# The first loads and the first matmuls of a gated attention and token-mixing kernel: another order of the DMA queues, another order of the first projection

## The chip, the cores and the metric

The kernel runs on one core of one Trainium2 chip. The metric is the device time of one execution in microseconds (us). A core has five engines with instruction streams of their own: TensorE (PE) multiplies matrices into the eight banks of PSUM, VectorE (DVE) and ScalarE (ACT) compute on SBUF and PSUM, GpSimd (POOL) does little here, and SyncE (SP) issues most of the DMAs. ACT issues DMAs as well. The engines wait for one another, and for DMAs, through semaphores.

## The reference

One input x of 2048 rows and 512 columns goes two ways, and a gate mixes the results. Way A is an attention with 32 heads of 16 columns, in which a row sees itself and seven earlier rows, two apart; way B is a layer norm and a two-layer perceptron over the rows (tokens) instead of the columns.

```python
def reference(A_x, A_wqkv, A_wo, B_x, B_w1, B_b1, B_w2, B_b2, gate_w):
    x = A_x
    g = sigmoid((x * gate_w).sum(-1, keepdims=True))
    # A: q, k, v = x @ wqkv, split in 32 heads of 16
    #    row s sees the rows s, s-2, ..., s-14: softmax(q . k / 4), times v, then @ wo
    # B: h = layernorm(x)
    #    u = gelu(einsum("bsd,sf->bdf", h, w1) + b1)
    #    y = (einsum("bdf,fs->bds", u, w2) + b2) transposed to (b, s, d)
    return g * a + (1 - g) * b
```

All inputs are bfloat16; wqkv is 512 x 1536, wo 512 x 512, w1 2048 x 1792, w2 1792 x 2048.

## The kernel before

The kernel first computes q, k and v with x transposed (XT, four blocks of 512 rows: block 0 to block 3) as the moving operand and columns of wqkv as weights. Then DVE multiplies q and shifted k (L690), PE sums over a head's columns (L698), ACT and DVE do the softmax, PE does the first layer of the perceptron (L812) and the second (L862), and at last the output projection wo (L878), after which DVE mixes both ways (L899) and SP stores.

Nothing loops on the chip. A list of operations is written out in Python (`A(engine, function, duration, reads, writes, ...)`, `sch.dma(queue, ...)`), and a small planner in the same file (`_Sched`) puts them in an order for each engine. It goes by the durations given, by priorities (`prio`), by dependencies from `reads` and `writes`, by `order` edges that fix an order without a wait, and for some DMAs by a time of landing that is given by hand (`lands`). From the order it works out the waits. So a DMA's `lands` and an operation's duration decide nothing on the chip but the order.

The stage that matters here is the first 15 us.

- **Columns 0 to 127 of block 0.** SP loads them as they lie (XP, `d_xp`, L479: 512 pieces of 256 bytes). PE transposes them by matmuls against an identity (`f_tr`, L545, operations `tr0` and `tr1`), ACT evicts one half (`ev_tra`, L555) and DVE the other (`ev_trb`, L557).
- **Columns 128 to 511 of block 0** come by a transposing DMA (`ld_xt0`, L473). Blocks 1 to 3 come by transposing DMAs of all four column quarters (`ld_xt`, L460).
- **The weights.** `ld_w(tn, d0, n, q)` (L447) loads n quarters (of 128 rows) of Wq, Wk or Wv (tn 0, 1, 2), from quarter d0 on, by queue q. ACT's queue issues Wq's quarters 0 and 1 as its first work, SP's the rest: after `d_xp` and the transposing DMA come Wq's quarters 2 and 3, Wk's 0 and 1 together, Wk's 2 and 3 together, X's tiles 0 and 1 (`ld_x`, L439, for the layer norm), block 1, and X's tiles 2 and 3. The later ones wait for the landing of a DMA some places ahead (`throttle`).
- **Warm-up.** While nothing has landed, PE multiplies constants: six matmuls of 512 columns and one of 256 (`f_warm`, L537) ahead of the transposes, and one of 512 behind them.
- **The first projection.** q and k of block 0 are eight tiles (four column groups each), in eight PSUM banks, and each is the sum of four matmuls, over the quarters d = 0 to 3 (`f_proj`, L619). Before, PE goes over the quarters for q's four banks first (16 matmuls), then for k's four banks (16 matmuls), two quarters of one bank at a time.
- **Evictions.** ACT evicts a bank as soon as its four quarters are summed: L627 for q, L630 for k and v. After block 0 the projections of blocks 1 to 3 use banks 0 to 3 in turn, so each has to be evicted before it is used again.
- **ACT's table.** ACT loads a function table (1.28 us) ahead of its first activation; before, that is `ev_tra`, behind the two DMA issues.
- **DVE** takes the statistics of X's tiles 0 to 3 (L574) ahead of its first product of q and k (L690), which needs q and k of blocks 0 and 1 for one column group. That order is written out (`chain`, L959).

Of the kernel before, what the change touches and what calls it, by code (L numbers as in the profile page):

```python
# [6 lines left out]
FP32 = mybir.dt.float32  # L7
U8 = mybir.dt.uint8
ALU = mybir.AluOpType
AF = mybir.ActivationFunctionType  # L10
# [3 lines left out]
D = 512  # L14
# [319 lines left out]
def bass_gated_mix__sliding_local_dilated__mixer_token_mlp__prompt_kernel(nc, A_x, A_wqkv, A_wo, B_x, B_w1, B_b1, B_w2, B_b2, gate_w, out, dbg=None):  # L334
    with contextlib.ExitStack() as es:
# [3 lines left out]
        sch = _Sched()  # L339
# [3 lines left out]
        wqkv_v = A_wqkv.rearrange("(dt p) c -> p dt c", p=128)  # L343
# [7 lines left out]
        WQKV = view("WQKV", BF16, [(3 * D, 4), (1, 3 * D)])  # L351
# [26 lines left out]
        def small(n):  # L378
            v_ = view("SMALL", FP32, [(1, n)], extra=so[0])
            so[0] += n  # L380
            return v_
# [5 lines left out]
        SD = small(NST)  # L387
# [14 lines left out]
        def col(v_, i):  # L402
            return bass.AP(v_.tensor, v_.offset + i, [list(v_.ap[0]), [1, 1]])
# [11 lines left out]
        A = sch.add  # L415
# [12 lines left out]
        def mk_dma(dst, src):  # L428
            return lambda e: e.dma_start(dst, src)

        init_dmas = []

        def throttle():
            return [init_dmas[-5]] if len(init_dmas) >= 5 else []

        def prev_dma():
            return [init_dmas[-1]] if init_dmas else []

        def ld_x(t0, n, q="sp"):  # L439
            ds = sch.dsem("x%d" % t0)  # L440
            op = sch.dma(q, mk_dma(X[:, t0:t0 + n, :], xv[:, t0:t0 + n, :]), n * 128 * D * 2, ds,
                         writes=["x%d" % t for t in range(t0, t0 + n)], deps=throttle() if q == "sp" else [], after=prev_dma() if q == "sp" else [], name="d_x%d" % t0)
            if q == "sp":
                init_dmas.append(op)
            return op

        def ld_w(tn, d0, n, q="sp"):  # L447
            ds = sch.dsem("wqkv%d_%d" % (tn, d0))
            op = sch.dma(q, mk_dma(WQKV[:, d0:d0 + n, tn * D:(tn + 1) * D], wqkv_v[:, d0:d0 + n, tn * D:(tn + 1) * D]),
                         n * 128 * D * 2, ds, writes=["wqkv%d_%d" % (tn, dt) for dt in range(d0, d0 + n)],  # L450
                         deps=throttle() if q == "sp" and n == 4 else [], after=prev_dma() if q == "sp" else [],
                         issue=0.65 if n == 4 else 0.45, name="d_wp%d_%d" % (tn, d0))
            if q == "sp":
                init_dmas.append(op)
            return op

        def ld_xt(sb):
            ds = sch.dsem("xt%d" % sb)
            dst = XT[:, :, sb * 512:(sb + 1) * 512]
            op = sch.dma("sp", lambda e: e.dma_start_transpose(dst, x2d[sb * 512:(sb + 1) * 512, :]), 512 * D * 2, ds,  # L460
                         writes=["xt_%d" % t for t in range(4 * sb, 4 * sb + 4)], deps=throttle(), after=prev_dma(), name="d_xt%d" % sb)
            init_dmas.append(op)
# [4 lines left out]
        def xt_of(sb, d0=0, d1=4):  # L467
            return XT0[d0:d1] + (XT0[4:] if d0 == 0 else []) if sb == 0 else ["xt_%d" % t for t in range(4 * sb, 4 * sb + 4)]

        def ld_xt0():  # L470
            ds = sch.dsem("xt0")
            dst = XT[:, 1:4, 0:512]
            op = sch.dma("sp", lambda e: e.dma_start_transpose(dst, x2d[0:512, 128:512]), 512 * 384 * 2, ds, issue=1.25,  # L473
                         writes=XT0[1:4], after=prev_dma(), name="d_xt0")
            init_dmas.append(op)
            return op

        XP = view("OUTS", BF16, [(128, 4), (1, 128)])
        d_xp = sch.dma("sp", mk_dma(XP, xv[:, 0:4, 0:128]), 512 * 128 * 2, sch.dsem("xp"), writes=["outs0"], issue=0.4, name="d_xp")  # L479
        d_xp.lands = 3.9  # L480
        init_dmas.append(d_xp)

        first_loads = [ld_w(0, 0, 1, "act"), ld_xt0(), ld_w(0, 1, 1, "act"), ld_w(0, 2, 1), ld_w(0, 3, 1), ld_w(1, 0, 2), ld_w(1, 2, 2),
                       ld_x(0, 2)]
        ld_xt(1)
        first_loads.append(init_dmas[-1])
        for op_, t_ in zip(first_loads, (3.5, 5.7, 5.0, 6.3, 6.7, 7.6, 8.6, 9.4, 11.0)):
            op_.lands = t_
            op_.deps.clear()
        first_loads[2].order.add(first_loads[0])  # L490
        init_dmas[:] = [first_loads[1]] + first_loads[5:]
        ld_x(2, 2)
        ld_x(4, 4)
        ld_xt(2)
# [6 lines left out]
        def ld_w1(j):  # L501
# [4 lines left out]
            if j < 4:  # L506
# [8 lines left out]
                       writes=["wo"], deps=throttle(), after=prev_dma(), name="d_wo")  # L515
# [4 lines left out]
        for i_, (v_, n_) in enumerate(((B_b1, NFT), (B_b2, NST))):  # L520
            vr = v_.rearrange("(t q j) -> q t j", q=4, j=32)
            for q_ in range(4):
                sch.dma("sp", mk_dma(psub(BR, 32 * q_, n_, 32 * i_, [(1, 32)]), vr[q_]), n_ * 64, ds_b, reads=["br"],
                        writes=["br_%d_%d" % (i_, q_)], deps=throttle(), after=prev_dma(), name="d_b_%d_%d" % (i_, q_), issue=0.45)
        d_w1.append(ld_w1(3))
        A("dve", lambda e: e.transpose(out=BT, in_=BR), 0.2, reads=["br_%d_%d" % (i_, q_) for i_ in range(2) for q_ in range(4)],
          writes=["btc"], name="t_b")
# [5 lines left out]
        def f_warm(n, w_=D):  # L533
            def fn(e):
                ins = None
                for _ in range(n):
                    ins = e.matmul(ps[:, 7, 0:w_], lhsT=CONE[:, 0:128], rhs=CONE[:, 0:w_], start=True, stop=True)  # L537
                return ins
            return fn

        def f_tr(h):
            def fn(e):
                ins = None
                for t in range(2):
                    ins = e.matmul(ps[:, 5 + h, 128 * t:128 * t + 128], lhsT=XP[:, 2 * h + t, :], rhs=IDENT, start=True, stop=True)  # L545
                return ins
            return fn

        A("pe", f_warm(6), 2.56, writes=["lg7_0", "lg7_1"], name="warm1", prio=-100)
        w2_ = A("pe", f_warm(1, 256), 0.2, writes=["lg7_0", "lg7_1"], name="warm2", prio=-100)  # L550
        ta_ = A("pe", f_tr(0), 0.215, reads=["outs0", "ident"], writes=["lg5_0", "lg5_1"], after=[w2_], name="tr0", prio=-100)
        tr_ = A("pe", f_tr(1), 0.215, reads=["outs0", "ident"], writes=["lg6_0", "lg6_1"], after=[ta_], name="tr1", prio=-100)
        A("pe", f_warm(1), 0.43, writes=["lg7_0", "lg7_1"], after=[tr_], name="warm3", prio=-100)
        w3_ = tr_
        A("act", lambda e: e.activation(out=XT[:, 0, 0:256], in_=ps[:, 5, 0:256], func=AF.Copy), 0.35, reads=["lg5_0", "lg5_1"],  # L555
          writes=["xt0_0"], name="ev_tra", prio=0)
        A("dve", lambda e: e.tensor_copy(out=XT[:, 0, 256:512], in_=ps[:, 6, 0:256]), 0.35, reads=["lg6_0", "lg6_1"],  # L557
          writes=["xt0_0b"], name="ev_trb", prio=0)

        JK = view("OUTS", BF16, [(1, D)], extra=0)  # L560
        def cols(v_, lo, n, step=1):
            return bass.AP(v_.tensor, v_.offset + lo * step, [list(v_.ap[0]), [step, n]])
# [4 lines left out]
        def mv(t0, k, w=1):  # L567
            return bass.AP(MV.tensor, MV.offset + 2 * t0 + k, [list(MV.ap[0]), [2, 8]] + ([[1, w]] if w > 1 else []))

        ln3_act = list(range(NST))  # L570
        for hf in range(2):
            t0 = 8 * hf
            for t in range(t0, t0 + 8):
# [19 lines left out]
                out=cols(NMR, t0_, 8), in0=mv(t0_, 0), scalar=-0.5, in1=cols(RSTD, t0_, 8),  # L593
# [38 lines left out]
        tnames = ["q", "k", "v"]  # L632
        first = [(tn, dl) for tn in range(2) for dl in range(4)]
        fbn = [["acc%d" % b] for b in range(4)] + [["lg%d_0" % b, "lg%d_1" % b] for b in range(4, 8)]
        for (b0, d0, d1, s0, s1) in ((0, 0, 1, 0, 512), (0, 1, 2, 0, 512), (0, 2, 3, 0, 512), (0, 3, 4, 0, 512), (4, 0, 2, 0, 512), (4, 2, 4, 0, 512)):
            for b in range(b0, b0 + 4):
                tn, dl = first[b]
                last_main[0] = A("pe", f_proj(tn, dl, 0, b, d0, d1, s0, s1), 0.216 * (d1 - d0) * (s1 - s0) / 512,
                                 reads=xt_of(0, d0, d1) + ["wqkv%d_%d" % (tn, dt) for dt in range(d0, d1)],
                                 writes=fbn[b], after=[last_main[0]], name="pf_%s%d_%d_%d" % (tnames[tn], dl, d0, s0))  # L640
                last_main[0].order.add(w3_)
        for b, (tn, dl) in enumerate(first):
            A("act", f_evq(tn, dl, 0, b), 0.52, reads=fbn[b] + (["k5pad"] if tn == 1 else []),
              writes=["%s5_%d_0" % (tnames[tn], dl)], name="ev_%s%d_0" % (tnames[tn], dl), prio=0)
# [7 lines left out]
        for (tn, dl, sb) in seq_proj:  # L652
# [4 lines left out]
                             writes=["acc%d" % bank], after=[last_main[0]], name="pj_%s%d_%d" % (tnames[tn], dl, sb), prio=0)  # L657
            A("act", f_evq(tn, dl, sb, bank), 0.62, reads=["acc%d" % bank] + (["k5pad"] if tn == 1 else ["v5pad"] if tn == 2 else []),
              writes=["%s5_%d_%d" % (tnames[tn], dl, sb)], name="ev_%s%d_%d" % (tnames[tn], dl, sb), prio=0)
# [11 lines left out]
                writes=["xa"] + ["wqkv%d_%d" % (tn, dt) for tn in range(3) for dt in range(4)], name="d_xa")  # L671
        for t in range(NST):
# [5 lines left out]
          writes=["th"], name="g_tanh", prio=0)  # L678
# [31 lines left out]
        for wh in range(2):  # L710
# [6 lines left out]
            for (dl, c0, nc_) in pieces:  # L717
# [5 lines left out]
                  writes=wr, name="qkm_%d_%d_%d" % (wh, dl, c0), prio=0)  # L723
            rd = sum([pbn(b_) for b_ in bufs], []) + PBX[wh] + ["rp"]
            for wl in range(4):
                qop = A("pe", f_qkr(list(enumerate(bufs)), (wl,)), 0.92, reads=rd, writes=["lg%d_0" % (4 + wl), "lg%d_1" % (4 + wl)],
                        name="qkr_%d_%d" % (wh, wl), prio=-100 + wl, delay=BURST_DELAY)
                A("act", (lambda wh_, wl_: (lambda e: e.activation(out=ATT[:, :, 4 * wh_ + wl_, :], in_=ps[:, 4 + wl_, :].rearrange("p (h c) -> p h c", h=2), func=AF.Copy)))(wh, wl),  # L728
                  0.55, reads=["lg%d_0" % (4 + wl), "lg%d_1" % (4 + wl)], writes=["lw%d" % (4 * wh + wl)],
                  name="lev_%d_%d" % (wh, wl), prio=0)  # L730
# [60 lines left out]
        for k_, u in enumerate(USEQ):  # L791
# [7 lines left out]
            for (nm, n_, du) in (("ava", 4, 2.25), ("avb", 2, 1.2)):  # L799
                A("dve", (lambda pv_, n__: (lambda e: e.tensor_tensor(out=pv_[:, 0:n__], in0=pv_[:, 0:n__], in1=pv_[:, n__:2 * n__], op=ALU.add)))(pv, n_),  # L800
                  du, writes=[pn], name="%s_%d" % (nm, u))
# [27 lines left out]
        for ft in range(NFT):  # L829
# [6 lines left out]
              name="gel_%d" % ft, prio=0)  # L836
# [84 lines left out]
        for i in range(NST):  # L921
# [4 lines left out]
            elif i > 1:  # L926
# [6 lines left out]
              name="t1_%d" % i, prio=0)  # L933
# [119 lines left out]
```

## Time and profile before

| what | us |
|---|---|
| median of 3 runs (lowest, highest) | 168.55 (168.44, 168.69) |
| the profiled execution, its own time | 168.55 |
| its span, from the first to the last instruction of the profile | 167.30 |
| PE busy in the span | 163.9 (98%) |
| DVE busy | 151.3 (90%) |
| ACT busy | 75.0 (45%) |
| matmuls of the projections (L619), 192 | 42.3 busy |
| matmuls of the first and of the second layer (L812, L862), 224 each | 48.7 busy each |
| DMA, moved over the whole span | 29.64 MB, 177 GB/s |

A profile comes from one execution. Times are from the start of the span. A group of instructions is named by the line of the kernel that issued it. Matmuls overlap in their pipeline, so the busy time of one (378 ns for 512 columns) is longer than the distance between the starts of two (0.2155 us in the steady part, 0.427 us at the start of the execution). The chain of waits is followed back from the last instruction, at each step to what released it. The landing of a DMA is the time at which its semaphore is complete; each DMA raises it in 16 steps, one for each DMA engine. These are the landings of the first DMAs before:

| DMA | issued by, at | landed |
|---|---|---|
| xp: plain columns 0 to 127 of block 0 | SP 0.80 | 3.91 |
| Wq quarter 0 | ACT 0.80 | 3.71 |
| Wq quarter 1 | ACT 1.26 | 4.31 |
| transposed columns 128 to 511 of block 0 | SP 1.29 | 5.73 |
| Wq quarter 2 | SP 2.99 | 6.11 |
| Wq quarter 3 | SP 3.59 | 6.45 |
| Wk quarters 0 and 1 | SP 4.08 | 7.44 |
| Wk quarters 2 and 3 | SP 4.55 | 8.39 |
| X tiles 0 and 1 | SP 5.07 | 9.05 |
| block 1, transposed | SP 5.58 | 11.04 |
| X tiles 2 and 3 | SP 8.87 | 11.93 |

### The profile page before, as it was taken

What the parts mean: (1) busy time and instruction counts of PE and PEld (TensorE: products, weight loads), DVE (VectorE), ACT (ScalarE), POOL (GpSimd) and SP (SyncE); (2) the same over time, 40 slices, a digit from 0 to 9 for tenths busy, and PEclk for the clock granted to TensorE, in tenths of its full rate; (3) what the DMA queues carried; (4) which work ended last, traced back from release to release, by engine and by line L of the source; (5) the groups of instructions that cost most, each with busy time, mean ns of one, the idle gap of its engine ahead of it and who ended that gap; (6) DMA issues with size and microseconds to landing.
All of it is one profiled execution on the core that took longest, in us unless ns stands there. A gap on an engine that the chain in (4) does not pass through costs nothing.

```text
span 167.3 us, 2152 instructions
## 1 busy us (share of the span) xinstructions
PE 163.9 (98%) x860; PEld 77.6 (46%) x860; DVE 151.3 (90%) x154; ACT 75.0 (45%) x116; POOL 0.7 (0%) x8
## 2 busy tenths in 40 slices
PE   7999999999999999999999999999999999999994
PEld 2455555554454444444444444444444444444463
DVE  0145999999999999999999999999999999999896
ACT  3077688889899818793113121131231321310100
POOL 1000000000000000000000000000000000000000
DMA  5999999968003837996579936462672580000454
GB/s 130 315 272 262 303 322 291 307 196 246 0 0 97 311 115 187 303 290 153 133 183 343 335 129 143 112 187 68 184 218 83 138 223 0 0 0 0 157 190 159
DMA packets 47625, 29.64 MB, mean 177 GB/s; under 512 B 9856, under 2 KB 46464, under 8 KB 47616
## 3 DMA queue, kind: packets, MB, share of 16 engines
q1 hardware_dynamic: 45504, 24.85, 54.0%
q10 hardware_dynamic: 2112, 4.66, 10.0%
q8 instruction: 7, 0.11, 0.3%
q14 instruction: 2, 0.02, 0.0%
HBM read 21.24 MB, written 2.10 MB: 140 GB/s over the span
## 4 chain that ended last, share of the span: by engine, by line
PE 94%; DVE 3%; DMA 2%; issue 0%
PE ps L812 29%; PE ps L862 29%; PE ps L619 25%; PE ps L878 6%; PE ps L698 4%; DVE arena L899 2%; DMA arena<-in_A_x_dram 2%; PE ps L545 0%; DVE arena L557 0%
## 5 line engine op out<-in xcount | busy, mean ns | idle before, releaser
L812 PE MATMUL ps<-arena 128*128 128x512 bf16 x224 | 48.7, 379 | 0.0
L862 PE MATMUL ps<-arena 128*128 128x512 bf16 x224 | 48.7, 379 | 0.0
L619 PE MATMUL ps<-arena 128*128 128x512 bf16 x192 | 42.3, 382 | 0.1
L690 DVE TENSOR_TENSOR arena<-arena 128x4096 bf16<-128x4096 bf16 (+1 forms) x12 | 35.5, 2996 | 2.3 <-ACT arena L630 1.8
L797 DVE TENSOR_TENSOR arena<-arena 128x8192 bf16<-128x8192 bf16 x8 | 35.0, 4419 | 0.0
L812 PEld LDWEIGHTS ps<-arena 128*128 128x128 bf16 x224 | 21.8, 98 | 26.7 <-ACT arena L728 0.4
L862 PEld LDWEIGHTS ps<-arena 128*128 128x128 bf16 x224 | 21.9, 98 | 26.5
L619 PEld LDWEIGHTS ps<-arena 128*128 128x128 bf16 x192 | 21.6, 114 | 20.8 <-DVE arena L557 0.7
L930 ACT ACTIVATE arena<-ps,arena 128x512 bf16<-128x512 f32 x16 | 12.4, 778 | 39.4 <-PE ps L862 39.4
L800 DVE TENSOR_TENSOR arena<-arena 128x4096 bf16<-128x4096 bf16 (+1 forms) x16 | 27.0, 1752 | 0.0
L630 ACT ACTIVATE arena<-ps 128x512 bf16<-128x512 f32 x32 | 18.5, 596 | 4.5 <-PE ps L619 4.5
L833 ACT ACTIVATE arena<-ps,arena 128x512 bf16<-128x512 f32 x14 | 9.6, 687 | 22.2 <-PE ps L812 17.4
L574 DVE BATCH_NORM_STATS2 arena<-arena 128x6 f32<-128x512 bf16 x16 | 10.0, 680 | 5.6 <-DMA arena<-in_A_x_dram 5.6
L878 PE MATMUL ps<-arena 128*128 128x512 bf16 (+1 forms) x80 | 14.2, 337 | 0.0
L899 DVE SCALAR_TENSOR_TENSOR arena<-ps,arena 128x512 bf16<-128x512 f32 (+1 forms) x20 | 11.5, 638 | 0.9 <-PE ps L878 0.7
L598 ACT ACTIVATE arena<-arena 128x512 bf16<-128x512 bf16 x16 | 12.2, 806 | 0.0
L627 ACT ACTIVATE arena<-ps 128x512 bf16<-128x512 f32 x16 | 9.0, 596 | 5.5 <-PE ps L619 5.4
L878 PEld LDWEIGHTS ps<-arena 128*128 128x128 bf16 x80 | 7.8, 98 | 6.3
L674 DVE SCALAR_TENSOR_TENSOR arena<-arena 128x512 bf16<-128x512 bf16 x16 | 10.1, 685 | 0.0
L744 DVE TENSOR_TENSOR arena<-arena 128x512 bf16<-128x512 bf16 (+4 forms) x11 | 7.3, 667 | 0.6 <-ACT arena L763 0.2
L698 PE MATMUL ps<-arena 128*32 128x512 bf16 x128 | 7.3, 380 | 0.0
L728 ACT ACTIVATE arena<-ps 128x512 bf16<-128x512 f32 x8 | 4.7, 592 | 4.6 <-PE ps L698 4.6
(42 smaller groups left out, 40.5 us busy)
## 6 DMA issues: line engine op xcount, KB each, us to landing
arena<-in_B_w_dram SPq DMA_DIRECT2D x7, 1024.0 KB, 8.3
arena<-in_B_w_dram SPq DMA_DIRECT2D x8, 896.0 KB, 5.1
arena<-arena ACTq DMA_DIRECT2D x32, 128.0 KB, 3.0
arena<-in_A_x_dram SPq DMA_DIRECT2D x4, 512.0 KB, 5.1
out_dram<-arena SPq DMA_DIRECT2D x14, 128.0 KB, 1.7
arena<-in_A_x_dram SPq DMA_DIRECT2D x1, 1536.0 KB, 7.9
arena<-in_A_wqkv_dram SPq DMA_DIRECT2D x2, 256.0 KB, 3.6
arena<-in_A_x_dram SPq DMA_DIRECT2D x2, 256.0 KB, 3.5
```

The lines of the kernel that those rows point to most:

```text
L598: A("act", (lambda t_: (lambda e: e.activation(out=X[:, t_, :], in_=X[:, t_, :], func=AF.Identity, scale=col(RSTD, t_), bias=col(NMR, t_)) ...
L619: ins = e.matmul(ps[:, bank, s0:s1], lhsT=lhsT, rhs=XT[:, dt, sb * 512 + s0:sb * 512 + s1], start=(dt == 0 and s0 == 0), stop=(dt == 3))
L630: return lambda e: e.activation(out=dst, in_=ps[:, bank, :], func=AF.Copy)
L690: return lambda e: e.tensor_tensor(out=PBL[buf][:, :, 512 * c0:512 * (c0 + nc_)], in0=in0, in1=in1, op=ALU.mult)
L698: ins = e.matmul(ps[32 * c:32 * c + 32, 4 + wl, :], lhsT=RP, rhs=PBL[buf][:, wl, c * 512:(c + 1) * 512], start=(dl == 0), stop=(dl == 3), ...
L797: A("dve", (lambda o_, i0, i1: (lambda e: e.tensor_tensor(out=o_, in0=i0, in1=i1, op=ALU.mult)))(pv, in0, in1), 4.4, reads=v_res + ["atx_% ...
L800: A("dve", (lambda pv_, n__: (lambda e: e.tensor_tensor(out=pv_[:, 0:n__], in0=pv_[:, 0:n__], in1=pv_[:, n__:2 * n__], op=ALU.add)))(pv, n ...
L812: ins = e.matmul(ps[:, bank, :], lhsT=W1W[:, slot, st, 128 * e_:128 * e_ + 128], rhs=X[:, st, :], start=(st == 0), stop=(st == NST - 1))
L862: ins = e.matmul(ps[:, bank, :], lhsT=W2S[slot][:, ft, 128 * e_:128 * e_ + 128], rhs=UT[:, ft, :], start=(ft == 0), stop=(ft == NFT - 1))
L878: ins = e.matmul(ps[:, bank, 0:c1 - c0], lhsT=OT[:, t, 128 * i:128 * i + 128], rhs=WO[:, t, c0:c1], start=(t == 0), stop=(t == 3))
L899: A("dve", (lambda i_, b_, c0_, c1_: (lambda e: e.scalar_tensor_tensor(out=T1[:, i_, c0_:c1_], in0=ps[:, b_, 0:c1_ - c0_], scalar=col(G, i ...
L930: A("act", (lambda i_, bank_: (lambda e: e.activation(out=T1[:, i_, :], in_=ps[:, bank_, :], func=AF.Identity, scale=col(OMG, i_), bias=co ...
```

## The change

- SP's queue begins with xp, then Wq's quarter 0 (from ACT's queue before), then the transposing DMA of block 0, then Wk's quarter 1, then quarter 2 of Wq and Wk in one DMA, quarter 3 of both in one DMA (`ld_qk`, new), block 1, X's tiles 0 and 1, X's tiles 2 and 3.
- ACT begins with an activation of one column (`pre`), which brings its table load with it, and then issues two weight loads, Wk's quarter 0 and Wq's quarter 1. The first of them waits for `pre` by semaphore.
- The 256-column warm-up matmul moves from ahead of the two transposes to behind them, behind the 512-column one.
- The first projection goes over all eight banks for quarter 0, then over all eight for quarter 1, then over q's four banks for quarter 2 and for quarter 3, then over k's four banks, two quarters of a bank at a time.
- The planner's times of landing are other ones.

On PE and DVE the kind and number of instructions stay the same, and the order changes only as told. On ACT the evictions of q and k of block 0 come in another order (q's first three, k's first, q's fourth, k's second and third), mixed with those of block 1.

```diff
-        d_xp.lands = 3.9
+
+        def ld_qk(d):
+            ds = sch.dsem("wqk%d" % d)
+            op = sch.dma("sp", mk_dma(WQKV[:, d, 0:2 * D], wqkv_v[:, d, 0:2 * D]), 2 * 128 * D * 2, ds,
+                         writes=["wqkv0_%d" % d, "wqkv1_%d" % d], after=prev_dma(), issue=0.45, name="d_wqk%d" % d)
+            init_dmas.append(op)
+            return op
+
         init_dmas.append(d_xp)
-
-        first_loads = [ld_w(0, 0, 1, "act"), ld_xt0(), ld_w(0, 1, 1, "act"), ld_w(0, 2, 1), ld_w(0, 3, 1), ld_w(1, 0, 2), ld_w(1, 2, 2),
-                       ld_x(0, 2)]
+        pre = A("act", lambda e: e.activation(out=col(SD, 0), in_=nc.const_aps.tensor(1.0, [128, 1], FP32), func=AF.Copy), 1.35,
+                writes=["sd0"], name="pre", prio=-100)
+        first_loads = [ld_w(0, 0, 1), ld_w(1, 0, 1, "act"), ld_w(0, 1, 1, "act"), ld_xt0(), ld_w(1, 1, 1), ld_qk(2), ld_qk(3)]
         ld_xt(1)
-        first_loads.append(init_dmas[-1])
-        for op_, t_ in zip(first_loads, (3.5, 5.7, 5.0, 6.3, 6.7, 7.6, 8.6, 9.4, 11.0)):
+        first_loads += [init_dmas[-1], ld_x(0, 2)]
+        for op_, t_ in zip(first_loads, (3.9, 4.5, 4.9, 6.2, 6.8, 7.5, 8.2, 10.8, 11.6)):
             op_.lands = t_
             op_.deps.clear()
-        first_loads[2].order.add(first_loads[0])
-        init_dmas[:] = [first_loads[1]] + first_loads[5:]
+        d_xp.lands = 3.1
+        first_loads[1].deps.add(pre)
+        first_loads[2].order.add(first_loads[1])
+        init_dmas[:] = [first_loads[3]] + first_loads[5:]
...
-        A("pe", f_warm(6), 2.56, writes=["lg7_0", "lg7_1"], name="warm1", prio=-100)
-        w2_ = A("pe", f_warm(1, 256), 0.2, writes=["lg7_0", "lg7_1"], name="warm2", prio=-100)
+        w2_ = A("pe", f_warm(6), 2.56, writes=["lg7_0", "lg7_1"], name="warm1", prio=-100)
...
-        w3_ = tr_
+        w3_ = A("pe", f_warm(1, 256), 0.2, writes=["lg7_0", "lg7_1"], after=[tr_], name="warm4", prio=-100)
...
-        for (b0, d0, d1, s0, s1) in ((0, 0, 1, 0, 512), (0, 1, 2, 0, 512), (0, 2, 3, 0, 512), (0, 3, 4, 0, 512), (4, 0, 2, 0, 512), (4, 2, 4, 0, 512)):
-            for b in range(b0, b0 + 4):
+        for (b0, nb, d0, d1, s0, s1) in ((0, 8, 0, 1, 0, 512), (0, 8, 1, 2, 0, 512), (0, 4, 2, 3, 0, 512), (0, 4, 3, 4, 0, 512),
+                                         (4, 4, 2, 4, 0, 512)):
+            for b in range(b0, b0 + nb):
```

## The prediction

> **What bounds the kernel now.** I read the chain of waits first, in order of time, then the timeline of the first 14 us, DVE's waits, and the table of one-microsecond stretches for the projection matmuls alone. The chain, with start and length in us:
>
> ```profile
> 0.80 3.10 DMA arena<-in_A_x_dram
> 3.91 0.14 issue
> 4.04 0.60 PE ps L545 x4
> 4.64 0.02 issue
> 4.66 0.44 DVE arena L557
> 5.10 0.05 issue
> 5.15 33.44 PE ps L619 x152
> ...
> 161.65 0.03 issue
> 161.68 3.98 DVE arena L899 x9
> ```
>
> From 5.15 to 161.65 it never leaves TensorE: nothing makes PE wait once the first projection matmul has started. The end is that start plus a fixed amount of PE work plus a tail that PE releases. The start hangs on one transfer, the 128 plain columns of x (xp, L479): lands at 3.91, is transposed on PE (L545), evicted by DVE (L557), and 5.15 follows. From landing to first matmul is 5.146 - 3.906 = 1.24 us.
>
> ```profile
> 0.80 1.02 ACTq L429 DMA_DIRECT2D arena<-in_A_wqkv_dram  x2
> 0.80 0.43 SPq L429 DMA_DIRECT2D arena<-in_A_x_dram  x1
> ...
> 0.84 2.93 PE L537 MATMUL ps<-const-bfloat16-1.0 128*128 128x512 bf16 x7 [0.84 <-PEq L1038]
> ...
> 1.29 1.64 SPq L473 DMA_TRANSPOSE arena<-in_A_x_dram  x1
> ...
> 1.84 1.28 ACT L555 ACT_TABLE_LOAD   x1 [1.84 <-issue]
> ```
>
> SP issues xp while ACT issues Wq's first quarter; the 16 DMA engines carry both. DVE is 90% busy, so whether it lets PE's gain through has to be asked; its later waits for others are these (us in total, times, longest):
>
> ```profile
> DVE arena L690 <- ACT arena L630: 1.8, 1, 1.8
> ...
> DVE arena L899 <- PE ps L878: 0.7, 1, 0.7
> ...
> DVE arena L690 <- PE ps L698: 0.4, 1, 0.4
> ```
>
> The 0.4 is at 42.2 and the 0.7 at 157.4, so DVE is 0.4 us and then 0.7 us ahead of PE, and its run starts at 15.08, when ACT has evicted k's first block-1 tile. It doesn't set the end.
>
> The stretch table (PE busy and count, PEld busy and count, granted clock, DMA share, GB/s):
>
> ```profile
> 5.00:6.00 1.00, 0.85 (x3) 0.31 (x4) 1.00 1.08 328
> 6.00:7.00 1.00, 1.00 (x6) 0.55 (x5) 1.00 1.05 259
> 7.00:8.00 1.00, 1.00 (x7) 0.49 (x6) 1.00 1.08 367
> ```
>
> The granted clock reads 1.00 throughout, but the first projection matmuls start at 5.146, 5.556, 5.982, 6.263, 6.479: 0.427 us apart, like the constant ones before them, then 0.281, then 0.2155. PE runs at half speed until about 6.11 (the 0.281 is 0.13 us of slow and 0.15 of fast). So of an earlier start half is lost, if this step stays where it is.
>
> **The change, part by part.** The profiled execution took 168.55 us (span 167.30 and 1.25 around it), which is the median of the three runs (168.44 to 168.69). Sums are made against it.
>
> *Wq's first quarter from ACT's queue to SP's, behind xp.* This is to give xp the engines alone. The trace's packet records: xp is 512 packets of 256 B; the first starts at 1.92, about 284 have started by 3.0, the last at 3.44; the receipt comes 0.46 later, at 3.906. Wq's 128 packets of 1 KB start at 2.24, 46 ns each, mostly between 2.6 and 3.3. While both run, xp gets 18 to 37 packets per 0.1 us; in the 0.2 us after Wq's are through, 77. But from 1.92 to 2.24, alone, it got only 14 to 40: there the start-up of the queue limits it. Bounds on xp's landing: 410 packets left at 2.3 at 77 per 0.1 us end at 2.83, landing 3.3; nothing gained, 3.906. Between: taking away only Wq's engine time, 128 x 46 ns / 16 = 0.37 us, gives 3.54. I take 3.4, between the first and the third.
>
> *The 256-column warm-up behind the transposes instead of ahead of them.* Before, PE is taken until 3.56; after, the six warm matmuls end at 3.35 and the transposes may start. From xp at 3.4 plus 0.135 they start at 3.535, the first projection at 3.535 + 1.105 = **4.64**, 0.51 earlier. (Floor: 3.35 + 1.105 = 4.46; ceiling: 5.15.) The two warm-ups behind them take 0.43 + 0.21 us after 0.38 us of transposes, 1.02 us in all, less than 1.105: hidden under the evictions. The matmul also needs Wq's first quarter: SP issues it at 1.24; the same load took 2.91 us from ACT, giving 4.15; even 3.3 us is in time.
>
> *What 0.51 us earlier is worth.* With the clock step at 6.11, (6.11 - 4.64) / 0.427 = 3.44 matmuls are slow instead of 2.26, each costing 0.21 more: 0.25 lost, **0.25 us kept**. Everything behind is PE's, so the end moves by it.
>
> *Deadlines of the other loads.* With 3.44 slow matmuls, matmul n starts at 6.11 + (n - 4.44) x 0.2155: the 5th (Wk's first quarter) at 6.23, the 9th (transposed columns, Wq's second) at 7.09, the 13th at 7.95, 17th 8.82, 21st 9.68, 33rd (block 1) 12.26. ACT's table load moves ahead of its two loads and they wait for the activation behind it: 0.80 + 1.30 + 0.21 (as at L587) + 0.05 = 2.36. ACT's queue holds nothing else but its half of the evictions, and it is free of issuing at about 3.4, before that. Issue to landing took 2.91 and 3.05, so 5.3 and 5.9: in time. The transposing DMA, passed by Wq's issue on SP, starts at about 1.69 instead of 1.29. Issue to landing was 4.44, so 6.13; with Wq's 0.37 us ahead of it in its queue and up to 0.37 more beside ACT's later loads, up to 6.9. The margin is 0.2 to 1.0 us; the nearest. The rest of SP's queue: one weight load of 128 KB at 3.4 and two of 256 KB, which landed 3.1 and 3.4 to 3.8 us after issue, so about 6.6, 7.4 and 8.1, each over 1 us early. Block 1 (landed 11.04) loses a 256 KB load ahead of it (0.66 us, as between 8.39 and 9.05): about 10.5 against 12.26.
>
> *X behind block 1.* X's tiles 0 to 3 land at about 11.1 and 11.9 (the bytes ahead of the last are the same), DVE's statistics on them end by 13.3, and DVE waits until 15.08 anyway: nothing. If that cover goes (landing after 13.8), DVE's 0.4 and 0.7 us of lead go first.
>
> *Eight banks.* As many matmuls, in another order. Banks 0 to 3 are complete at the 21st matmul instead of the 13th, so ACT's first eviction starts at 10.1 instead of 8.62, and its evictions follow back to back, 0.49 apart. k's first block-1 tile is the tenth: 14.5 to 15.1, so DVE starts at 15.1 as before, while PE is 0.25 ahead; the 0.41 covers that. Bank 1 is wanted at 13.1 and is free at 11.2: no wait of PE.
>
> Sum: 168.55 - 0.25 = **168.3 us**. Its own range is 168.2 (floor start, 0.34) to 168.45.
>
> **The skill, weighed.** The trace shows full speed from 6.11, with PE idle for 0.48 and 0.30 us between 3.56 and 5.15. The Trainium skill, "TensorE: Matmul & The Clock Gate", Part 1 (the clock gate), says that full speed is granted at the end of a free-running window of about 3.4 us that was busy, whatever was issued. By that the window ending at 6.11 began near 2.70, the one before it was about half empty, and filling PE's two gaps brings no earlier step. Free-running would also mean a new phase in every run; three runs within 0.25 us speak against much of that here.
>
> **Rivals.** (1) The clock step comes at another time, above all earlier, because PE is busy without gaps. Before, PE had 6.11 - 0.84 - 0.78 = 4.5 us of busy time before the step; if busy time counts, it now comes at 0.84 + 4.5 + 0.18 = 5.5 and half of 0.6 is gained on top: 168.0, and 167.85 from the floor start. For: the gaps go. Against: one trace cannot tell busy time from a fixed moment.
> (2) The change doesn't do what it says: xp's start-up, not Wq, sets its landing (14 to 40 packets per 0.1 us while alone), or a stall of a few tenths eats the gain. 168.45 to 168.6.
> (3) Slower: the transposing DMA comes too late. Place: the 9th matmul, wanted at 7.09. Price: 1 us per us. It eats the gain at 7.34 and makes the kernel slower by over 0.34 us from 7.68; it would need 6.0 us from issue where it took 4.44, though the later transposing DMAs, of four column blocks and behind more traffic, took 4.2 to 5.8. About 169.0.
>
> **How the numbers follow.** Forecast 0.42, rival (1) 0.27, (2) 0.19, (3) 0.12. About 0.2%, 0.34 us, is what a measurement of this kernel can tell from no change, so faster means under 168.21. About a third of the forecast's chance (0.14) lies there, and all of (1): faster 0.41. The rest of it and (2): same 0.47. (3): slower 0.12. Range 167.85 to 168.6: leaves out (3) and the edge of (1).
>
> **What would show it.** Right: xp lands near 3.4, the transposes (L545 before) start near 3.5, the first projection matmul near 4.64, the step from 0.427 to 0.2155 us stays near 6.1, no gap in PE until the tail. Wrong: xp at 3.9 (2); the step near 5.5 (1); a gap ahead of the 5th or 9th matmul (3), or ahead of the 33rd; DVE's lead at 42.2 gone.

## The result and the profile after

The changed kernel is slower by 0.65%: 169.63 us median of ten runs (168.68 to 171.77) against 168.41 (167.86 to 168.82) of ten runs of before beside it; ratio 1.0065, 95% interval 1.0039 to 1.0091. Ratios, here and below, leave out runs over 1.5% above the fastest of their kernel, of these ten 171.31 and 171.77. The profiled execution took 169.08 us, its span 167.8 against 167.3.

The chain of waits after, in order of time (start, length, what; L627 is the projection, L619 before):

```profile
0.80 0.45 SPq L429
1.25 0.06 issue
1.31 0.49 SPq L429
1.80 0.05 issue
1.85 5.88 DMA arena<-in_A_x_dram
7.72 0.14 issue
7.86 6.43 PE ps L627 x29
...
162.17 0.02 issue
162.19 3.98 DVE arena L908 x9
```

The path no longer begins with xp but with SP's issues of xp and of Wq's quarter 0, and then the transposing DMA of block 0, which is in flight for 5.88 us, where it was 4.44. PE starts its 9th projection matmul at 7.86, 0.14 after that landing; before it was at 7.34. The chain leaves PE at 162.17 instead of 161.65. So 0.52 us at the 9th matmul are 0.52 us at the end, and nothing behind it gives any back.

What PE waited for in the first 16 us after (us in total, times, longest; PEld is its weight load):

```profile
PEld ps L627 <- DMA arena<-in_A_wqkv_dram: 1.7, 2, 1.1
...
PE ps L627 <- DMA arena<-in_A_x_dram: 0.6, 1, 0.6
```

The weight-load rows overlap with PE's own work, so the stall is read from PE's row and the starts: the first eight matmuls start from 4.55 to 6.88, the 9th could follow at 7.1, and PE stands until 7.86. The early start did come: xp landed at 3.12 instead of 3.91. It was worth nothing, because the eight matmuls that it brought forward ended in front of a transfer that had become 2.0 us later (7.72 against 5.73). It was not the only late one: the 5th matmul, at 6.20, had just got Wk's quarter 0 (6.16), and Wq's quarter 1, which the 9th needs too, landed at 7.49. With the transposing DMA alone in time, the 9th would still have started after the 7.34 of before.

The stretches in which that DMA's packets move, of all engines (start and end, length, PE, PEld, DVE, ACT, POOL busy with counts, granted clock, DMA share, GB/s; the DMA share is the packets' time over that of 16 engines, and passes 1 where packets overlap). Before:

```profile
3.40:4.40 1.00, 0.73 (x6) 0.39 (x5) 0.00 (x0) 0.00 (x0) 0.00 (x0) 1.00 1.22 288
4.40:5.40 1.00, 0.91 (x5) 0.21 (x3) 0.42 (x1) 0.38 (x1) 0.00 (x0) 1.00 1.29 321
```

After:

```profile
3.40:4.40 1.00, 1.00 (x7) 0.53 (x5) 0.38 (x1) 0.38 (x1) 0.00 (x0) 1.00 0.93 168
4.40:5.40 1.00, 1.00 (x5) 0.34 (x4) 0.04 (x1) 0.00 (x0) 0.00 (x0) 1.00 1.16 185
```

The last two columns are where to look. From 4.4 to 5.4 the DMA engines are nearly as busy as before (1.16 against 1.29) and move 42% less. The pair alone proves little: `e10_behind_eviction` below reads 1.15 and 196 GB/s in the same stretch with no packet of ACT's beside the transposing ones, since those end at 5.04 and the stretch goes on into the next loads.

The packet records tell the two apart. Before, the transposing DMA's 256 B packets, alone, went at about 113 per 0.1 us and 18 ns each. After, ACT's two loads run beside them from 3.55 on, and the transposing packets go at 20 to 84 per 0.1 us until 5.9, taking 17 to 42 ns in the mean of a 0.2 us slice, while ACT's own packets of 1 KB (46 ns alone) take 47 to 206 ns in most such slices. Both stall: from 4.8 to 6.0 only 22 of ACT's 256 packets start, none of them after 5.6, and the transposing packets are slow until 5.9 all the same.

### The profile page after: what moved, and what is told of

It is laid out like the page before. It is cut to its first block, busy times and chain, and to the rows that moved or that the text cites. A ratio compares the mean times of both kernels' runs of the same rounds, so it can differ in the third digit from the quotient of the medians.

```text
span 167.8 us, 2139 instructions
## 1 busy us (share of the span) xinstructions
PE 163.2 (97%) x846; PEld 77.7 (46%) x860; DVE 151.2 (90%) x154; ACT 75.0 (45%) x117; POOL 0.7 (0%) x8
## 4 chain that ended last, share of the span: by engine, by line
PE 91%; DMA 4%; DVE 2%; issue 1%; SPq 1%
PE ps L871 29%; PE ps L821 29%; PE ps L627 24%; PE ps L887 6%; PE ps L707 4%; DMA arena<-in_A_x_dram 4%; DVE arena L908 2%; SPq L429 1%
## 5 line engine op out<-in xcount | busy, mean ns | idle before, releaser
L627 PE MATMUL ps<-arena 128*128 128x512 bf16 x188 | 42.3, 383 | 1.0 <-DMA arena<-in_A_x_dram 0.6
L627 PEld LDWEIGHTS ps<-arena 128*128 128x128 bf16 x192 | 21.5, 114 | 22.0 <-DMA arena<-in_A_wqkv_dram 1.7
L638 ACT ACTIVATE arena<-ps 128x512 bf16<-128x512 f32 x32 | 18.8, 599 | 3.5 <-PE ps L627 3.4
L635 ACT ACTIVATE arena<-ps 128x512 bf16<-128x512 f32 x16 | 9.3, 602 | 8.3 <-PE ps L627 8.3
L737 ACT ACTIVATE arena<-ps 128x512 bf16<-128x512 f32 x8 | 4.7, 592 | 4.6 <-PE ps L707 4.6
```

What stands on the lines that cost most here:

```text
L627: ins = e.matmul(ps[:, bank, s0:s1], lhsT=lhsT, rhs=XT[:, dt, sb * 512 + s0:sb * 512 + s1], start=(dt == 0 and s0 == 0), stop=(dt == 3))
L638: return lambda e: e.activation(out=dst, in_=ps[:, bank, :], func=AF.Copy)
```

## The experiments

Theory C, contention: the transposing DMA is late because ACT's loads run beside it. Rival L, lateness: it is late because Wq's quarter 0 goes ahead of it on SP. Line numbers differ by a few between the kernels. The diffs show the lines that matter; the planner's landing times and order edges were fitted to them.

### The loads taken away from beside the transposing DMA

`e1_act_at_once`, ACT's loads without the wait:

```diff
-        pre = A("act", lambda e: e.activation(out=col(SD, 0), in_=nc.const_aps.tensor(1.0, [128, 1], FP32), func=AF.Copy), 1.35,
-                writes=["sd0"], name="pre", prio=-100)
...
-        first_loads[1].deps.add(pre)
```

> The changed kernel without the one-column activation and the wait on it: ACT issues Wk's quarter 0 and Wq's quarter 1 at 0.8 and 1.3 us, as its two loads were issued before the change; the table load comes behind them. Everything else is the changed kernel's. Theory C (contention: the block-0 transposing DMA was late because ACT's two loads, issued at 2.3 and 2.8, run beside its packets): the loads are through before its packets get going, issue to landing comes back from 5.9 to 4.4 to 4.7 us, it lands at 6.2 to 6.6, the 9th matmul starts by 7.2, xp lands at 3.3 to 3.9 because it shares the engines again; time within 0.3 us of before. Theory L (lateness: it is late because SP issues Wq's quarter ahead of it and that quarter lies ahead of it in the queue): it still lands at 7.3 to 7.8 and the time is 0.4 to 1.2 us above before.

`e2_sp_behind`, ACT's loads on SP, behind the transposing DMA:

```diff
-        first_loads = [ld_w(0, 0, 1), ld_w(1, 0, 1, "act"), ld_w(0, 1, 1, "act"), ld_xt0(), ld_w(1, 1, 1), ld_qk(2), ld_qk(3)]
+        first_loads = [ld_w(0, 0, 1), ld_xt0(), ld_w(1, 0, 1), ld_w(0, 1, 1), ld_w(1, 1, 1), ld_qk(2), ld_qk(3)]
```

> The changed kernel with ACT's two loads issued by SP instead, right behind the block-0 transposing DMA, in the same queue; ACT keeps the one-column activation. Theory C: nothing runs beside the transposing DMA any more, so although it is issued at 1.85, it lands 4.1 to 4.5 us later, at 5.9 to 6.4; then the two loads are last, at about 6.6 and 7.1, the 5th matmul waits for the first of them, and the time is 0.2 to 0.7 us above before. Theory L: it lands at 7.3 or later, the loads behind it later still, and the time is over 1 us above before.

`e3_sp_ahead`, one of them ahead of it and one behind:

```diff
+        first_loads = [ld_w(0, 0, 1), ld_w(1, 0, 1), ld_xt0(), ld_w(0, 1, 1), ld_w(1, 1, 1), ld_qk(2), ld_qk(3)]
```

> The changed kernel with ACT's two loads on SP: Wk's quarter 0 ahead of the block-0 transposing DMA, Wq's quarter 1 behind it. The transposing DMA is issued 0.5 us later still, at about 2.35, with one load more ahead of it in its queue, and nothing beside it. Theory C: 4.3 to 4.6 us from issue to landing, so 6.6 to 7.0; Wk's quarter 0 lands near 4.8; the 9th matmul starts near 7.1 to 7.3; time 0.3 us below to 0.1 above before. Theory L: the lateness grows with the issue and with what lies ahead: landing at 8.2 or later, time over 1 us above before.

| kernel | transposing DMA: issued, landed, in flight | ratio to before, 95% interval |
|---|---|---|
| before | 1.29, 5.73, 4.44 | |
| the change | 1.85, 7.72, 5.88 | 1.0065 (1.0039 to 1.0091) |
| `e1_act_at_once` | 1.86, 6.10, 4.24 | 0.9991 (0.9977 to 1.0005) |
| `e2_sp_behind` | 1.85, 5.64, 3.79 | 1.0022 (1.0007 to 1.0036) |
| `e3_sp_ahead` | 2.32, 6.36, 4.04 | 1.0017 (1.0003 to 1.0031) |

All three keep Wq's quarter ahead of the transposing DMA and its late issue, and in all three it is in flight for no longer than before. L asked for a landing at 7.3 us or later (8.2 in `e3_sp_ahead`) and falls. In `e3_sp_ahead` it is issued later still, with one load more ahead of it, and lands 1.4 us earlier than in the change. The landings came 0.1 to 0.3 us earlier than C had put them, and `e3_sp_ahead` took 0.24 us more than before (medians) where C allowed 0.1. The row of that DMA (L473) in the change, then in `e2_sp_behind`:

```profile
DMA to landing us min/median/max: 5.9/5.9/5.9
```

```profile
DMA to landing us min/median/max: 3.8/3.8/3.8
```

`e2_sp_behind` and `e3_sp_ahead` lose their gain elsewhere: with all weight loads on SP's queue, some come late. In `e2_sp_behind` the 5th matmul waits for Wk's quarter 0 (6.29) and the 17th for quarter 2 (9.36); in `e3_sp_ahead` the 9th waits for Wq's quarter 1 (7.05) and the 17th for quarter 2 (8.98). `e1_act_at_once` has no such wait, but xp shares the engines again and lands at 3.96.

### The order on SP put back

`e5_tr_ahead`:

```diff
+        first_loads = [ld_xt0(), ld_w(1, 0, 1, "act"), ld_w(0, 1, 1, "act"), ld_w(0, 0, 1), ld_w(1, 1, 1), ld_qk(2), ld_qk(3)]
```

> The changed kernel with the block-0 transposing DMA ahead of Wq's quarter 0 on SP, as before the change; ACT's two loads stay behind the one-column activation, at 2.3 and 2.8. Theory C: the loads still run beside it, and issue to landing stays over 5.2 us: 6.5 to 7.2. Theory L: issue at 1.3 and landing at 5.7 to 6.0, as before the change. In both Wq's quarter 0 now lands at 6.1 or later and holds up the first matmul, so the time is 0.3 to 1.0 us above before and does not tell the theories apart; the landing does.

Landing 5.80, in flight 4.49: L's number, and a miss for C as I had put it. The packet records show why. ACT's loads were issued at 2.33 and 2.74 as in the change, but their first packet moved only at 4.37 (in the change at 3.55), when 1,433 of the transposing DMA's 1,536 packets had started, at 110 to 114 per 0.1 us from 3.6 on. There was little overlap. So C has to be said of packets, not of issues. Why ACT's packets waited 2.0 us after their issue here and 1.2 in the change, no run tells.

The time was 171.38 us, ratio 1.0181 (1.0157 to 1.0205), more than the 0.3 to 1.0 us that I expected. Wq's quarter 0 landed at 6.50, so the first matmul started at 6.64 instead of 5.15; and behind that idle time PE stayed at half speed until about 9.3, seven matmuls long.

### The loads added beside it, in the kernel before

`e8_before_beside`, before with Wq's quarters 2 and 3 on ACT:

```diff
-        first_loads = [ld_w(0, 0, 1, "act"), ld_xt0(), ld_w(0, 1, 1, "act"), ld_w(0, 2, 1), ld_w(0, 3, 1), ld_w(1, 0, 2), ld_w(1, 2, 2),
+        first_loads = [ld_w(0, 0, 1, "act"), ld_xt0(), ld_w(0, 1, 1, "act"), ld_w(0, 2, 1, "act"), ld_w(0, 3, 1, "act"), ld_w(1, 0, 2), ld_w(1, 2, 2),
```

> The kernel before with one thing added: Wq's quarters 2 and 3, which SP issues behind the block-0 transposing DMA, are issued by ACT behind its two loads, at about 1.8 and 2.3, so that they run beside the transposing DMA's packets. Theory C: the transposing DMA, issued at 1.3 as before, lands at 6.3 or later instead of 5.7, and if it is past 6.4 the 5th matmul waits. Theory L (issue and position in the queue): unchanged at 5.6 to 5.9, since nothing changes on SP ahead of it. Time: 0 to 0.8 us above before under C, within 0.2 under L.

This is the strongest answer. Nothing ahead of the transposing DMA changes on SP, it is issued at 1.31, and it lands at 8.92, far past the 5.6 to 5.9 of L. Its row, what PE waited for, and two stretches as above:

```profile
DMA to landing us min/median/max: 7.6/7.6/7.6
```

```profile
PE ps L621 <- DMA arena<-in_A_x_dram: 2.9, 1, 2.9
```

```profile
3.40:4.40 1.00, 0.60 (x7) 0.27 (x5) 0.00 (x0) 0.59 (x1) 0.00 (x0) 1.00 1.09 210
4.40:5.40 1.00, 0.70 (x6) 0.26 (x4) 0.42 (x1) 0.38 (x1) 0.00 (x0) 1.00 1.23 126
```

Again the engines are busy (1.23) and move little: 126 GB/s where before moved 321. The transposing packets took 29 to 67 ns each from 4.4 to 5.4, in the means of 0.2 us slices. Median 171.16 us, 2.63 above before's 168.53, ratio 1.0103 (1.007 to 1.0136), beyond what C expected; the spread of its eleven runs, 169.28 to 174.0, suggests that the slowing is unsteady, though only one of them has a trace.

### The time of ACT's loads

`e6_pool_wait` and `e9_dve_wait` let them wait for a small operation of GpSimd or DVE instead of the activation, `e10_behind_eviction` puts them behind ACT's first eviction:

```diff
-        first_loads[1].deps.add(pre)
+        first_loads[1].deps.add(c_v5)
...
+        first_loads[1].deps.add(c_rp)
...
+        first_loads[1].order.add(c_ev)
```

The three added lines belong to the three kernels in that order; `c_v5` is GpSimd's memset at L421, `c_rp` DVE's reduction at L424, `c_ev` the eviction `ev_tra`. In the first two `pre` is left out.

> The changed kernel, but ACT's two loads wait for a small memset of GpSimd that ends near 1.35, not for an activation behind the table load (which goes, so that the table load follows the loads). They are issued at about 1.4 and 1.9: late enough to leave the engines to xp, early enough to be through before the packets of the block-0 transposing DMA. Theory C, now said more narrowly (the transposing DMA is slowed while packets of another queue run beside its own, whenever the DMAs were issued): xp lands at 3.0 to 3.3, the first matmul starts at 4.5 to 4.7, the transposing DMA lands 4.1 to 4.5 us after its issue at 1.85, at 6.0 to 6.4, no gap ahead of the 5th or 9th matmul; time 0.2 to 0.6 us below before. Rival D (the transposing DMA's lateness varies from run to run and has nothing to do with ACT's loads): landing at 7 or later, time above before.

> The changed kernel, but ACT's two loads wait for DVE's first reduction, which ends at 1.5, and no longer for an activation behind the table load; the table load follows them. They are issued at about 1.5 and 2.0, between the 1.0 of the last such run (no slowing) and the 2.3 of the change (slowed). Theory C: packets start about 1.3 us after the issue, near 2.9, when xp's are through, and the second load's overlap the first of the transposing DMA's (from 3.2). If the overlap at its start is enough, it lands at 7.0 or later and the time is 0.3 us or more above before; if only a longer overlap slows it, it lands at 6.0 to 6.6, the first matmul starts at 4.55, nothing waits, and the time is 0.2 to 0.6 us below before.

> The changed kernel with ACT's two loads behind ACT's first eviction, so issued at about 4.1 and 4.6 instead of 2.3 and 2.8, still on ACT's queue. Theory C (slowed by packets beside its own): their packets start near 5.3, when the transposing DMA's are through (5.0 in the runs without slowing), and it lands at 5.6 to 6.1. Rival Q (loads on ACT's queue delay the transposing DMA whenever they come behind it): 7 or later. In both the loads land late, at about 7.0 and 7.4, the 5th matmul waits for the first of them, and the time is 0.5 to 1.2 us above before.

| kernel | ACT's loads issued | transposing DMA in flight, landed | first matmul | ratio, 95% interval |
|---|---|---|---|---|
| `e1_act_at_once` | 0.80, 1.25 | 4.24, 6.10 | 5.00 | 0.9991 (0.9977 to 1.0005) |
| `e6_pool_wait` | 0.97, 1.39 | 4.17, 6.02 | 4.92 | 1.0003 (0.9978 to 1.0028) |
| `e9_dve_wait` | 1.53, 1.95 | 4.98, 6.83 | 4.97 | 0.998 (0.9966 to 0.9995) |
| the change | 2.32, 2.79 | 5.88, 7.72 | 4.55 | 1.0065 (1.0039 to 1.0091) |
| `e10_behind_eviction` | 3.81, 4.23 | 3.70, 5.54 | 4.54 | 1.0076 (1.005 to 1.0103) |

The time in flight rises as the loads come closer to the transposing packets, and falls back when they come after them: ACT's queue as such (rival Q) does no harm. `e6_pool_wait` missed its issue time, since the planner moved the memset to 0.80; so xp was not left alone (it landed at 3.68), and its first matmul and its time are near those of `e1_act_at_once`. In its trace 82 of ACT's packets ran between 3.64 and 4.04 among the first transposing ones, which kept their 18 ns: a short overlap did no harm there. Two of its twelve runs took 169.77 and 169.93 against the median of 168.51; without a trace of them, what slowed them is open. `e9_dve_wait` shows the slowing start and end in one trace. Its two stretches (columns as above):

```profile
4.40:5.20 0.80, 0.45 (x3) 0.15 (x2) 0.04 (x1) 0.00 (x0) 0.00 (x0) 1.00 1.23 173
5.20:6.00 0.80, 0.80 (x5) 0.34 (x4) 0.00 (x0) 0.00 (x0) 0.00 (x0) 1.00 1.27 289
```

Until ACT's last packets have gone, near 4.9, 173 GB/s; then, alone, 289, with engines as busy. Its landing, 6.83, lies between the two that had been expected. It takes 0.2% less than before, the most of all kernels here, though its interval overlaps that of `e1_act_at_once`: xp alone (3.20), and the 9th matmul at 6.97, after a wait of 0.1. It doesn't get all that xp offers: Wq's quarter 0 lands at 4.88, beside ACT's loads, and holds the first matmul until 4.97. In `e10_behind_eviction` the 5th matmul waits for Wk's quarter 0 until 7.39.

### The change again, its bank order, and `e1_act_at_once` again

> The changed kernel itself once more, for a second trace, since its times spread over 1.5 us where those of before spread over 1.0. Theory C: both ACT loads again run beside the block-0 transposing DMA, which lands 5.5 us or more after its issue, and the 9th matmul starts right behind that landing (0.1 to 0.15 us); the end lies as much later than in the first profile as that matmul does. Rival D: a landing near 6.0 to 6.5 in this trace.

> The changed kernel with the bank order of before: q's four banks over all four quarters, then k's four. It then wants the transposed columns at the 5th matmul instead of the 9th, four full-speed matmuls (0.86 us) earlier. If the late transposing DMA is what costs time, the end comes 0.7 to 0.9 us later than with eight banks for the same landing: 0.4 to 0.6% above the changed kernel. If the eight banks themselves cost time (evictions later, DVE started later), it comes nearer to before than the changed kernel does.

> The kernel of the first experiment (ACT's two loads at once, no wait) once more, for a second trace and a second set of times: its median was 0.37 us below before, its interval reached from -0.23% to +0.05%. Theory C: no slowing again, landing of the transposing DMA 6.0 to 6.5, no gap ahead of the 5th and 9th matmul; the time is 0 to 0.4 us below before. Where PE's step to full speed falls differs from run to run (before 4.1 to about 6.6 in the traces so far), which alone moves the time by up to 0.8 us.

`r2_after_again` is the changed kernel unedited. The slowing is there (in flight 6.04, landed 7.89), but the 9th matmul did not follow that landing: this time Wk's quarter 0 suffered as well, landed at 7.28 instead of 6.16, and the 5th matmul waited for it. Its chain:

```profile
2.32 4.95 DMA arena<-in_A_wqkv_dram
7.28 0.05 issue
7.32 32.14 PE ps L627 x148
```

The 9th matmul started at 8.22, 0.35 later than in the first profile, and the execution took 169.43 us, 0.35 more. Either partner of the contention can be the one that PE waits for, which may be why the median of the change lies above its first profile.

Rival D falls with the traces together. In eight of the thirteen, at most 82 of ACT's packets start between the first and the last transposing packet, and the transposing DMA is in flight for 3.70 to 4.49 us; in `e9_dve_wait` it is 116 and 4.98 us; in the other four (the change twice, `e4_four_banks`, `e8_before_beside`) 220 to 271 and 5.88 to 7.61 us. A slower DMA also catches more packets, so the count goes with the edits and doesn't replace them.

`e4_four_banks` puts the change's loop back to before's order (q's four banks over all quarters first):

```diff
-        for (b0, nb, d0, d1, s0, s1) in ((0, 8, 0, 1, 0, 512), (0, 8, 1, 2, 0, 512), (0, 4, 2, 3, 0, 512), (0, 4, 3, 4, 0, 512),
+        for (b0, nb, d0, d1, s0, s1) in ((0, 4, 0, 1, 0, 512), (0, 4, 1, 2, 0, 512), (0, 4, 2, 3, 0, 512), (0, 4, 3, 4, 0, 512), (4, 4, 0, 2, 0, 512),
```

Landing 7.80, 5th matmul at 7.94; 170.01 us in the profiled execution against 169.08 of the change, 0.93 more, and 1.0119 (1.0082 to 1.0157) of before. That is the four matmuls (0.86) and the 0.08 by which the 5th matmul starts later here than the 9th in the change: the eight banks are worth what was worked out, and no cost of them shows.

`e11_act_at_once_2`: landing 6.21, no gap, 168.32 us median, ratio 0.9986 (0.9972 to 0.9999). Two sets of runs, 0.9991 and 0.9986: a gain of 0.1%, if any, over before.

## Why the prediction was wrong

- **xp alone.** Right, and more: landing 3.12 where I took 3.4 and set the bound at 3.3. The slow start is there with xp alone as well: 20 to 35 packets per 0.1 us from 1.92 to 2.2. But then they went at 88 to 101 per 0.1 us in the means of 0.2 us slices, not at 77: in the 0.2 us of before from which I took the 77, another 20 packets of ACT's loads moved, so xp was not alone there. The first matmul started at 4.55 (predicted 4.64), the transposes at 3.35, the floor.
- **The transposing DMA.** This is the step that failed: "Issue to landing was 4.44, so 6.13; with Wq's 0.37 us ahead of it in its queue and up to 0.37 more beside ACT's later loads, up to 6.9." Wq's quarter ahead costs nothing that shows (`e2_sp_behind`: 3.79 in flight). Of the 1.6 us between 6.13 and 7.72, 0.16 came from the issue (1.85, not 1.69) and 1.44 from the time in flight. The loads beside it cost not the 0.37 us of their own engine time but 1.4 us and more (5.88 and 6.04 in flight against 3.70 to 4.49 in the runs in which little or nothing went beside it). I added up engine times, and no row of before had a transposing DMA with another queue's packets beside it for longer than 0.25 us. A cost that no row showed was given a sum of busy times as its upper bound.
- **The rival of that name.** Its place (the 9th matmul) and its price (1 us per us) were right: 0.52 late there, 0.52 late at the end. Its chance, 0.12, came from the same sum. "About 169.0" was near the profile, 169.08, and 0.6 below the median, 169.63; the range ended at 168.6.
- **The other loads.** Wk's quarter 0 was to land at 5.3 and did at 6.16 and 7.28; Wq's quarter 1 at 5.9, and did at 7.49 and 7.70. It is the same error: the loads are held up as the transposing DMA is. What lies behind them on SP came 0.4 to 1.4 us later than predicted, still in time.
- **Half of an earlier start is lost to the clock.** The arithmetic stands, the fixed moment does not. In the profiled run of the change, full speed came near 6.2, as predicted. But `e2_sp_behind`, `e3_sp_ahead` and `r2_after_again` do the same work on PE until 4.55, to 0.01 us, and go to full speed near 4.6, 5.8 and 4.8. The stretch 4.4 to 5.4 for the projection alone (columns: PE, PEld, granted clock, DMA share, GB/s), `e2_sp_behind` and then `e3_sp_ahead`:

```profile
4.40:5.40 1.00, 0.85 (x4) 0.37 (x4) 1.00 1.05 225
```

```profile
4.40:5.40 1.00, 0.85 (x3) 0.33 (x4) 1.00 1.11 226
```

  Four matmuls against three, with the granted clock at 1.00 in both. So neither a fixed moment nor busy time (rival 1) sets the step; it has another phase in every run. The Trainium skill's rule of a free-running window ("TensorE: Matmul & The Clock Gate", Part 1) fits this; no trace shows the window itself. I set it aside on three runs within 0.25 us; ten runs of before spread over 0.96.
- **Eight banks, X behind block 1.** Right in that neither cost anything that shows. `e4_four_banks` shows the gain of the first. X's tiles landed at 12.12 and 12.86, 1.0 later than worked out, and DVE's run started at 15.60, behind ACT's evictions; the end moved by PE's 0.52 alone.
- **A gain had been there.** With xp alone and no load beside the transposing DMA's main part, the gain is 0.2% (`e9_dve_wait`), near the forecast's 0.25 us. That is no proof of the forecast: the first matmul there started at 4.97, not 4.64, and the phase of the clock step moves single runs by more than the gain.

## What to carry to other kernels

When a transfer is moved, ask which packets will run beside it on another queue, and don't price that by adding engine time: look for a stretch of the profile in which both kinds run together, and where there is none, leave the range open on the slow side. A DMA share near its old value with fewer GB/s is a reason to look at the packets; here such a stretch stood for contention in one kernel and for a change of loads in another. And an earlier start is worth only what the next deadline leaves of it: move the loads behind it with the same care as the one on the path.

## What the runs showed of the hardware

- A transposing DMA (384 KB, 256 B packets) with plain loads of another queue beside it was late by more than the loads' own engine time, and the loads were late too: 3.7 to 4.5 us in flight without, 5.0 with two loads beside its start, 5.9 to 6.0 with two beside more of it, 7.6 in the kernel with four loads on ACT. Packets that take 18 ns alone take up to 67 in the mean of 0.2 us. Plain loads beside a plain load lost less: in `e1_act_at_once` xp and Wk's quarter landed at 3.96 and 3.47, and before xp and Wq's quarter at 3.91 and 3.71, against 3.12 for xp alone. Slow transposing packets also occur with no other queue's packets beside them, for shorter: 19 to 41 ns from 4.0 to 4.8 in `e3_sp_ahead`, behind a load of SP's own, and 26 ns from 4.6 to 5.0 in `e11_act_at_once_2`. So other packets make the slowing long, and are not its only condition. What in the DMA engines makes the packets take longer, no run here tells.
- The step of PE to full speed fell before 4.2 in two traces, and near 4.6, 4.8, 5.3, 5.8, 6.1, 6.2 and 6.6 in others with nearly the same warm-up, and at 9.3 behind 2.0 us of idle PE. By half of the slow time this moves one execution by several tenths of a us, which may be much of the spread between runs of one kernel (0.96 us in ten runs of before).
